# A chunked recurrence with an MLP behind it: another form of the products, three products on GpSimd, all DMAs on SP

## The chip, the cores and the metric

The kernel runs on one core of one Trainium2 chip. The metric is the time of one execution on the device in microseconds, as the median of several runs. A profile of one execution gives the time of each instruction. Its engines are PE (TensorE, matrix products; PEld is its weight load), DVE (VectorE), ACT (ScalarE), POOL (GpSimd) and SP (SyncE, which here only issues DMAs).

## What is computed

Thirty-two heads (4 batches times 8) carry a 40x40 state through 768 steps; the outputs then go through an MLP.

```python
for t in range(S):
    y[:, :, t] = np.einsum('bhd,bhde->bhe', rt, state)
    Sa = np.einsum('bhde,bhe->bhd', state, at)
    state_decay = state * wt[:, :, None, :] - np.einsum('bhd,bhe->bhde', Sa, bt)
    state = state_decay + np.einsum('bhd,bhe->bhde', vt, kt)
...
h = x @ w_in                      # x: [3072, 320], w_in: [320, 2048]
g = h * np.tanh(softplus(h))
out = g @ w_out                   # [2048, 320]
```

## The kernel before

**Chunks.** The 768 steps are cut into 12 chunks of 64 (`C`). Inside a chunk the decays `w` are taken out by running products: `P` (forward) multiplies `a`, `E` (backward, of reciprocals) multiplies `b` and `k`. What is left is a triangular system per head: with A the strictly triangular products of `a` and `b`, and T the inverse of (1 + A), the vectors u = Sa of the whole chunk come from one product with T. The 32 heads lie as two halves (`al`, `be`) on the partitions (0 to 39 and 64 to 103) and eight (`s`) along the row, or as two groups `g` of the recurrence.

**Preparation** (`pre_a`, lines 126 to 203) runs once per chunk and `be`, 24 units in all. SP loads `wa` (decays and `a` in one tile) and `bk`. DVE reduces, inverts and scans (L145 to L157), multiplies `a` by P (L152) and `b`, `k` by E (L170). ACT spreads `a` into block-diagonal `ad` (L155). PE multiplies `bk` by `ad` (L186); ACT evicts the parts into `GP` (L188, L189) and `HA` (L190), DVE masks one part into `HA` (L191) and masks `GP` (L193). PE transposes `bk` (L202). A small product rearranges the chunk's decays into `RW` (L166). POOL stores P (L172).

**Inversion** runs once per pair of chunks. `pre_inv` (L205 to L221) inverts the 32x32 blocks on DVE: a transpose, a loop of 30 steps with a product (L214) and a sum (L216), two more transposes (L218, L220). `post_inv` (L223 to L260) builds the 64x64 inverse from the blocks with 32x32 products (L232, L241), writes it block-diagonally into `bdT` with ACT copies (L249 to L251) and multiplies it into `HA` (L258), evicted as `KT` (L260). T is thus multiplied into the chunk's matrices before the state is known.

**Recurrence.** `step(c)` runs, for two groups g: `step_a` copies the state into `VS` (L279) and gets u in one product with `KT` (L286), evicted into `UVT` (L288); `step_u` transposes u into `UVQ` (L294 with TensorE's transpose, L296 as a product with the identity, L300); `step_d` transposes the state (L310); `step_b` multiplies `UVT` with block-diagonal `r` (`bdr`, L320) and masks into `UVQ` (L322); `step_c` forms outputs and the new state (L340, L345, L348 to L352). Loads of a chunk (`step_loads`, L265 to L273) are into single buffers and are issued behind the chunk before.

**MLP** (`Mlp.run`): 12 blocks of 256 tokens, four quarters each: `mlp1` (L591, L593, L596, L597) and, `LAG` = 3 quarters behind, `mlp2` (L611 to L613). Its weights come as 64-bit numbers and are converted by ACT and DVE (L459 to L469, L500, L501). With `NO1` = 3, three of the eight `w_out` tiles are loaded ahead of the end of the attention and the others after it, when its memory is free.

**Order.** A planner orders the instructions of each engine: by default those written first go first, those that can go are not held back by those that can't, and `high_priority(offset=...)` (the table `OFF`) moves a block forward or back. `ORDER` says in which order the steps of a pair ('0', '1'), the inversion of the next pair ('i') and the preparation two pairs ahead ('a') are written. `QS` names the engines that issue the DMAs: "SGGG" is SP for the loads of the preparation and POOL for step loads, output stores and stores of P. Each engine and each queue runs its list strictly in order.

Of the kernel before, what the change touches and what calls it, by code (L numbers as in the profile page):

```python
# [15 lines left out]
NHA = 8  # L16
# [3 lines left out]
NKT = 2  # L20
# [7 lines left out]
QS = "SGGG"  # L28
NU = 2
NBR = 1  # L30
NAD = 2
# [4 lines left out]
ORDER = '0aiA1'  # L36

OFF = {'I': 80, 'T1': 80, 'P00': -40, 'P10': 80, 'P11': 40, 'b0': 15, 'c0': 600, 'u0': -15, 'u1': 250, 'd0': 250,
       'd1': 150, 'W': 600, 'V': 400, 'E': 150, 'I0': 600, 'I1': -15, 'I2': 15, 'I3': 150, 'I4': 80, 'p4': 15,
       'I5': -150, 'J5': 600, 's0': 150, 's2': -15, 's3': 80, 's4': 250, 's6': -15, 's7': -40, 's8': 150, 's10': -150}  # L40
SORD = 'a0 b0 u0 d0 a1 b1 u1 d1 c0 c1'
# [6 lines left out]
def layouts(inp, S=768):  # L48
# [7 lines left out]
    wt = w.transpose(4, 2, 1, 6, 3, 0, 5).reshape(nch, 2, 2, 40, 8, C)  # L56
    wa = np.zeros(wt.shape[:4] + (1040,), np.float32)
    wa[..., :520].reshape(wt.shape[:4] + (8, 65))[..., 1:] = wt
    wa[..., 528:] = a.transpose(4, 2, 1, 6, 3, 0, 5).reshape(nch, 2, 2, 40, 512)
    o['wa'] = wa  # L60
    bt, kt = (x.transpose(4, 2, 1, 6, 3, 0, 5).reshape(nch, 2, 2, 40, 8, 1, C) for x in (b, k))
    bk = np.concatenate([bt, kt], -2)
    bk[:, 1] = np.concatenate([kt, bt], -2)[:, 1]
    o['bk'] = bk.reshape(nch, 2, 2, 40, 8, 128)
    o['rD'] = np.ascontiguousarray(r.transpose(4, 1, 6, 2, 3, 0, 5)).reshape(nch, 2, 40, 16, C)
    o['vD'] = np.ascontiguousarray(vv.transpose(4, 1, 6, 3, 0, 2, 5)).reshape(nch, 2, 40, 8, 128)
    o['vN'] = np.ascontiguousarray(vv.transpose(4, 2, 5, 3, 0, 1, 6)).reshape(nch, 2, C, 16, 40)
    p = np.arange(128)
    cst = np.zeros((128, 328), np.float32)
    cst[:, :128] = np.eye(128)  # L70
    cst[:, 128:192] = (p[:, None] % 64) < np.arange(64)
    cst[:, 192:256] = np.arange(64) < (p[:, None] // 64) * 32 + p[:, None] % 32
    cst[:, 256:296] = (p[:, None] % 64) == np.arange(40)
    cst[:, 296:328] = np.arange(32) < p[:, None] % 32
# [4 lines left out]
def attention(ctx, tc, I, yD, pD, nch, M):  # L79
# [11 lines left out]
    ci = pool("ci", 1, ictx)  # L91
# [4 lines left out]
    cst = cs.tile([128, 328], F32, name="cst")  # L96
    ident = cst[:, 0:128]
    maskQ = cst[:, 128:192]
    maskH = cst[:, 192:256]
    maskG = cst[:, 296:328]  # L100
    wab = [cp.tile([128, 1040], F32, name=f"wa{i}") for i in range(NWA)]
    bkb = [cp.tile([128, 8, 168], F32, name=f"bk{i}") for i in range(NWA)]
    adb = [cp.tile([128, 8, 2, 2, 32], F32, name=f"ad{i}") for i in range(NAD)] * (2 // NAD)
    d1 = cp.tile([128, 584], F32, name="d1")
    bdT = [ci.tile([128, 8, 2, 64], F32, name=f"bdT{i}") for i in range(2)]
    z = cs.tile([128, 1], F32, name="z")
    V.memset(z, 0.0)
    for w, b in zip(wab, bkb):
        V.memset(w, 1.0)
        G.memset(b, 0.0)  # L110
    for t in [d1] + [x.rearrange("p s k a t -> p (s k a t)") for x in adb[:NAD]]:
        A.copy(t, z.broadcast_to(t.shape))
    for t in bdT:
        G.memset(t, 0.0)
    VS = [cs.tile([128, 2, 344], F32, name=f"VS{be}") for be in range(2)]
    UVT = cs.tile([128, 8, 256], F32, name="UVT")
    UVQ = [cs.tile([128, 16, 104], F32, name=f"UVQ{be}") for be in range(2)]
    bdr = [cs.tile([128, 2, 8, 2, 64], F32, name=f"bdr{i}") for i in range(NBR)] * (2 // NBR)
    ST = [cs.tile([128, 8, 64], F32, name=f"ST{g}") for g in range(2)]
    for t in VS + [UVT] + bdr[:NBR] + ST:  # L120
        G.memset(t, 0.0)

    RW, W2, HA, BKN, GP, KT = {}, {}, {}, {}, {}, {}
    LQ, SQ, OQ, PQ = (dict(S=SP, G=G, A=A)[x] for x in QS)

    def pre_a(c, be):
        n = 2 * c + be
        wa, bk, ad = wab[n % NWA], bkb[n % NWA], adb[n % 2]
        for al in range(2):
            q = slice(al * 64, al * 64 + 40)  # L130
            LQ.dma_start(out=wa[q], in_=I['wa'][c, be, al])
# [255 lines left out]
    def inv(n):  # L387
        with at(tc, 'I%d' % n), at(tc, 'I'):
            TT, T1 = pre_inv(n)
# [276 lines left out]
```

## Time and profile before

| what | value |
|---|---|
| median of 3 runs | 859.57 us (859.17 to 859.66) |
| the profiled execution | 858.42 us |
| its span, first to last instruction | 856.6 us |
| mean granted TensorE clock | 0.95 of full speed |
| busy: PE, DVE, ACT, POOL | 769.2, 466.2, 429.8, 123.5 us |

The time is a little longer than the span, as it includes what lies around the first and last instruction. Busy times add up the moments in which an engine works on something. A row of the groups reads: line, engine, operation, output<-inputs, shapes, count, then busy time in us and the mean of one in ns, then the idle time of the engine before them and what ended it. A busy PE is not PE at its peak, since products overlap; their pace is read from how many start in a stretch.

### The profile page before, as it was taken

To read this page: it belongs to the slowest core of one execution; us is meant where nothing else is said; L and a number is where in the kernel's file an instruction comes from. 1 tells how busy PE (TensorE), PEld (TensorE's weight loads), DVE (VectorE), ACT (ScalarE), POOL (GpSimd) and SP (SyncE) were. 2 spreads that over 40 slices of the span, in tenths; PEclk is the share of its full clock that TensorE was granted. 3 is DMA by queue.
4 is the path that set the end of the run, shared out by engine and by line. 5 is a ranking of instruction groups with operands and counts; after the bars stand their busy time and mean duration, and the time that the engine had idled before them with its cause. 6 is when DMAs were issued, how large, how long until landed. Compare 5 with 4: busy or idle time off the path is not lost.

```text
span 856.6 us, 19033 instructions
## 1 busy us (share of the span) xinstructions
PE 769.2 (90%) x7904; PEld 695.8 (81%) x7904; DVE 466.2 (54%) x975; ACT 429.8 (50%) x937; POOL 123.5 (14%) x206
## 2 busy tenths in 40 slices
PE   2545899899999999998798989999999999999998
PEld 2434777777778777876776889999999999999998
DVE  6789869758758856878663728422221222222110
ACT  4533647674564686557557626433333333333331
POOL 8100022233123213321212200000000000000000
PEclk9855699999979999999899999999999999999999
DMA  5622224443232334423425746201211121100000
GB/s 165 156 70 62 84 56 90 97 115 92 68 103 80 96 86 110 102 64 101 117 81 130 187 97 184 60 18 36 53 39 30 38 54 34 34 20 17 16 1 31
DMA packets 59750, 65.87 MB, mean 77 GB/s; under 512 B 25920, under 2 KB 49472, under 8 KB 59664
## 3 DMA queue, kind: packets, MB, share of 16 engines
q1 hardware_dynamic: 49296, 40.94, 17.2%
q0 software_dynamic: 10368, 23.72, 11.7%
q8 instruction: 62, 1.02, 0.5%
q14 instruction: 24, 0.20, 0.1%
HBM read 52.72 MB, written 11.86 MB: 75 GB/s over the span
## 4 chain that ended last, share of the span: by engine, by line
PE 59%; ACT 9%; DVE 3%; DMA 3%; issue 1%; SPq 0%; DVEq 0%; ACTq 0%
PE ph L591 19%; PE po L611 6%; PE po L612 6%; PE po L613 6%; PE pq L320 3%; PE pa L258 3%; PE pu L296 3%; PE pq L340 2%; PE pa L186 2%; PE pu L294 2%; PE pu L286 2%; PE pq L345 2%; DMA cv_d<-in_wo 2%; PE pu L310 1%; PE pa L202 1%
## 5 line engine op out<-in xcount | busy, mean ns | idle before, releaser
L591 PE MATMUL ph<-xh,w_ih 128*128 128x256 f32 x576 | 148.8, 284 | 0.0
L593 ACT ACTIVATE g<-ph 128x512 f32<-128x512 f32 x96 | 57.1, 597 | 179.0 <-PE ph L591 178.8
L597 DVE TENSOR_TENSOR gl<-g,gh 128x1024 fp32r<-128x1024 f32 x48 | 58.6, 1225 | 160.1 <-ACT gh L596 159.8
L186 PE MATMUL pa<-bk,ad 128*128 128x168 f32 x384 | 86.0, 374 | 46.5 <-DVE bk L170 16.7
L591 PE MATMUL ph<-xh,w_il 128*128 128x256 f32 x576 | 124.0, 283 | 0.0
L611 PE MATMUL po<-w_oh,gh 128*128 128x320 f32 x384 | 118.1, 310 | 1.5 <-ACT w_oh L500 1.5
L612 PE MATMUL po<-w_ol,gh 128*128 128x320 f32 x384 | 118.7, 309 | 0.0
L613 PE MATMUL po<-w_oh,gl 128*128 128x320 f32 x384 | 118.4, 309 | 0.0
L186 PEld LDWEIGHTS pa<-bk,ad 128*128 128x128 f32 x384 | 70.4, 232 | 52.9 <-issue 25.7
L591 PEld LDWEIGHTS ph<-xh,w_ih 128*128 128x128 f32 x576 | 109.5, 190 | 0.2 <-issue 0.2
L591 PE MATMUL ph<-xl,w_ih 128*128 128x256 f32 x384 | 100.6, 284 | 0.0
L591 PEld LDWEIGHTS ph<-xh,w_il 128*128 128x128 f32 x576 | 96.5, 191 | 0.2 <-issue 0.2
L611 PEld LDWEIGHTS po<-w_oh,gh 128*128 128x128 f32 x384 | 71.9, 188 | 2.2 <-ACT w_oh L500 2.2
L591 PEld LDWEIGHTS ph<-xl,w_ih 128*128 128x128 f32 x384 | 73.2, 191 | 0.1
L612 PEld LDWEIGHTS po<-w_ol,gh 128*128 128x128 f32 x384 | 72.2, 188 | 0.1
L613 PEld LDWEIGHTS po<-w_oh,gl 128*128 128x128 f32 x384 | 72.2, 188 | 0.0
L258 PE MATMUL pa<-bdT,HA 128*104 128x128 f32 x384 | 54.1, 294 | 10.4 <-ACT bdT L251 8.2
L216 DVE TENSOR_TENSOR XL<-XL,tmp 128x30 f32<-128x30 f32 (+9 forms) x180 | 59.0, 328 | 2.6
L214 DVE TENSOR_TENSOR tmp<-XL 128x30 f32<-128x30 f32 (+9 forms) x180 | 58.4, 324 | 2.5
L258 PEld LDWEIGHTS pa<-bdT,HA 128*104 128x104 f32 x384 | 47.5, 182 | 14.8 <-ACT bdT L251 9.5
L320 PE MATMUL pq<-bdr,UVT 128*128 128x128 f32 x384 | 51.1, 284 | 2.8 <-DVE UVQ L322 2.3
L596 ACT CAST gh<-g 128x1024 fp32r<-128x1024 f32 x48 | 50.1, 1047 | 1.1
(92 smaller groups left out, 1310.9 us busy)
## 6 DMA issues: line engine op xcount, KB each, us to landing
wa<-in_wa SPq DMA_DIRECT2D x48, 162.5 KB
bk<-in_bk SPq DMA_DIRECT2D x48, 160.0 KB
cv_d<-in_wi SPq DMA_DIRECT2D x12, 512.0 KB
cv_d<-in_wo SPq DMA_DIRECT2D x8, 640.0 KB
pD<-P POOLq DMA_DIRECT2D x48, 81.2 KB, 2.6
VS<-in_vN POOLq DMA_DIRECT2D x24, 160.0 KB, 3.1
UVT<-in_vD POOLq DMA_DIRECT2D x24, 160.0 KB, 3.8
bdr<-in_rD POOLq DMA_DIRECT2D x24, 160.0 KB, 4.9
```

What stands on the lines that cost most here:

```text
L186: PE.matmul(pt[:, j], ad[:, s0 + j].rearrange("p k a t -> p (k a t)"), bk[:, s0 + j], start=(j == 0), stop=True, skip_group_check=True)
L214: V.tensor_tensor(out=tv, in0=X[:, i + 1:32, i:i + 1].broadcast_to([128, 31 - i, i]), in1=X[:, i:i + 1, 0:i].broadcast_to([128, 31 - i, i] ...
L216: V.tensor_tensor(out=X[:, i + 1:32, 0:i], in0=X[:, i + 1:32, 0:i], in1=tv, op=ALU.add)
L258: PE.matmul(pk[:, j], ha[:, s0 + j], bd[:, s0 + j].rearrange("p a t -> p (a t)"), start=(j == 0), stop=True, skip_group_check=True)
L320: PE.matmul(pq[:, s], UVT[:, g * 4 + s, be * 128:be * 128 + 128], br[:, be, g * 4 + s].rearrange("p a t -> p (a t)"), start=(s == 0), stop ...
L591: PE.matmul(o, w, x, start=(j == 0 and n == 0), stop=(n == 7), skip_group_check=True)
L593: A.activation(g[:, f0:f0 + 2], ph, AF.Mish)
L596: A.copy(gh, g)
L597: V.tensor_tensor(out=gl, in0=g, in1=gh.bitcast(F32), op=ALU.subtract)
L611: PE.matmul(po[k], gh[:, j, t], oh, start=(f == 0), stop=False, skip_group_check=True)
L612: PE.matmul(po[k], gh[:, j, t], ol, start=False, stop=False, skip_group_check=True)
L613: PE.matmul(po[k], gl[:, j, t], oh, start=False, stop=(f == 15), skip_group_check=True)
```

## The change

T is no longer multiplied into the chunk's matrices beforehand. `step_a` multiplies the state with `HT` (a by P and the masked products) to W, and `step_u` then multiplies W with T (`TF`), once for u in one layout and once in the other; the transposes of `step_u`, `bdT`, `KT`, `HA`, `ad` and the product for `RW` go. In preparation and in `step_b` the block-diagonal operands go as well: each product uses one half of the partitions (64 rows). DVE's masks of the preparation go from three to two a unit. Products of `a` with P, of `b`, `k` with E and the mask of `GP` move from DVE to POOL, as do copies and clears of `TF`. All DMAs are issued by SP. `OFF` keeps three entries, `ORDER` is '01iaA' (both steps, then inversion, then preparation), and `NO1` is 0: no `w_out` tile is loaded ahead.

```diff
-NO1 = 3
+NO1 = 0
-QS = "SGGG"
+QS = "SSSS"
-ORDER = '0aiA1'
-OFF = {'I': 80, 'T1': 80, 'P00': -40, 'P10': 80, 'P11': 40, 'b0': 15, 'c0': 600, 'u0': -15, 'u1': 250, 'd0': 250,
...
-SORD = 'a0 b0 u0 d0 a1 b1 u1 d1 c0 c1'
+ORDER = '01iaA'
+OFF = {'W': 600, 'V': 400, 'E': 150}
+SORD = 'a0 u0 b0 d0 a1 u1 b1 d1 c0 c1'
...
 # pre_a(c, al)
-        V.tensor_tensor(out=a3, in0=a3, in1=P3[:, :, 0:64], op=ALU.mult)
-        for al in range(2):
-            q = slice(al * 64, al * 64 + 64)
-            A.copy(ad[q, :, :, al], a[q].rearrange("p (s k t) -> p s k t", k=2, t=32))
...
-        V.tensor_tensor(out=bk4, in0=bk4, in1=E3[:, :, 0:64].unsqueeze(2).broadcast_to([128, 8, 2, 64]), op=ALU.mult)
+        for be in range(2):
+            a = ht[hb[be], al, :, be]
+            G.tensor_tensor(out=a, in0=a, in1=P3[hb[be], :, 0:64], op=ALU.mult)
+        bk4 = bk.rearrange("p s (x t) -> p s x t", x=2)
+        G.tensor_tensor(out=bk4, in0=bk4, in1=E3[:, :, 0:64].unsqueeze(2).broadcast_to([128, 8, 2, 64]), op=ALU.mult)
...
-                PE.matmul(pt[:, j], ad[:, s0 + j].rearrange("p k a t -> p (k a t)"), bk[:, s0 + j], start=(j == 0), stop=True,
-                          skip_group_check=True)
...
+        pt = [ps_g.tile([128, 8, 64], F32, name="pa") for _ in range(2)]
+        for s in range(8):
+            for be in range(2):
+                PE.matmul(pt[be][:, s], bk[hb[be], s], ht[hb[be], al, s, be], start=(s == 0), stop=True, skip_group_check=True)
+        for be in range(2):
+            q0, q1 = slice(be * 64, be * 64 + 32), slice(be * 64 + 32, be * 64 + 64)
+            A.mul(gp[q0], pt[be][q0].rearrange("p s (k t) -> p s k t", k=2)[:, :, ::-1], -1.0)
+            A.mul(gp[q1, :, 1], pt[be][q1, :, 32:64], -1.0)
+            V.tensor_tensor(out=ht[hb[1 - be], al, :, be], in0=pt[be][hb[1 - be]],
+                            in1=mask[hb[1 - be]].unsqueeze(1).broadcast_to([64, 8, 64]), op=ALU.mult)
+        G.tensor_tensor(out=gp[:, :, 1], in0=gp[:, :, 1], in1=maskG.unsqueeze(1).broadcast_to([128, 8, 32]), op=ALU.mult)
...
 # pre_inv, behind the loop of L211
+        V.transpose(tf[:, :, 0:32].rearrange("p u t -> p t u"), X)
+        V.transpose(gp[:, :, 1], tf[:, :, 0:32])
+        for be in range(2):
+            q1 = slice(be * 64 + 32, be * 64 + 64)
+            G.tensor_copy(tf[q1, :, 32:64], tf[q1, :, 0:32])
+            G.memset(tf[q1, :, 0:32], 0.0)
...
 # step_loads
+            SQ.dma_start(out=UVT[h * 64:h * 64 + 40, 2 * h:2 * h + 31:2], in_=I['vD'][c, h])
+            SQ.dma_start(out=rT[c % 2][h * 64:h * 64 + 40], in_=I['rT'][c, h])
+            if c > 0:
+                SQ.dma_start(out=bdr[c % 2][h * 64:h * 64 + 40, :, :, h].rearrange("p b s t -> p (b s) t"), in_=I['rD'][c, h])
...
 # step_a
+        for u in range(8):
+            for be in range(2):
+                PE.matmul(pu[hb[be], u], HT[c % NHT][:, u % 2, g * 4 + u // 2, be], VS[be][:, g, u * 40:u * 40 + 40],
+                          start=(u == 0), stop=True, skip_group_check=True)
+        A.mul(W[g][:, 0:320].rearrange("p (u d) -> p u d", d=40), pu, -1.0)
...
 # step_u
+        for u in range(8):
+            t = u0 + u % 2 * 8 + u // 2
+            for be in range(2):
+                PE.matmul(pt[hb[1 - be], u], W[g][hb[be], u * 40:u * 40 + 64], tf[hb[be], t], start=(u == 0), stop=True,
+                          skip_group_check=True)
+            if not last:
+                for be in range(2):
+                    PE.matmul(pn[hb[be], u], tf[hb[be], t], W[g][hb[be], u * 40:u * 40 + 40], start=(u == 0), stop=True,
+                              skip_group_check=True)
+        A.copy(UVT[:, g * 16 + 1:g * 16 + 17:2], pt)
+        if not last:
             for be in range(2):
+                A.copy(UVQ[be][hb[be], g * 8:g * 8 + 8, 64:104], pn[hb[be]])
...
 # step_b
+                t = 2 * (g * 8 + u) + 1 - be
+                PE.matmul(pq[be][:, u], UVT[hb[1 - be], t:t + 2].rearrange("p a t -> p (a t)"), r[hb[1 - be], g * 8 + u],
+                          start=(u == 0), stop=True, skip_group_check=True)
```

`HT` is four buffers, one per chunk, into which the loads put `a` directly; `TF` is two, one per pair. The recurrence's `step_c` and `step_d` are the same products with other index orders.

More of the change, by code (lines that the diff above doesn't have):

```diff
@@ L14 @@
 C = 64
-NHA = 8
+NHT = 4
+NTF = 2
 NBKN = 8
@@ L94, in attention @@
     pw = pool("pw", 2, pctx, "right")
-    cst = cs.tile([128, 328], F32, name="cst")
+    cst = cs.tile([128, 224], F32, name="cst")
     ident = cst[:, 0:128]
[L98 to L103, printed above, removed]
+    mask = cst[:, 128:192]
@@ L288, in step_a @@
[L288 to L297 removed]
+                A.copy(VS[be][srow[be], g].rearrange("p (s d) -> p s d", d=40), st[srow[be], :, 0:40])
@@ L536, in first @@
             self.w_in(wp, cv, range(NQ0, NQ1))
-        if NQ1 == 4:
-            self.mpx = self.pool("mpx", 2)
     def second(self):
```

247 lines of the change are left out of this document (90 added, 157 removed).

## The prediction

> **What bounds the kernel now.** I read the stretches of busy time by stage first, then the chain of waits, then the groups of instructions. The columns are: length, busy time of TensorE, its weight load, DVE, ACT and POOL, the granted clock of TensorE, share and rate of the DMA engines.
>
> ```profile
> span 856.6 us, 19033 instructions
> 0.00:104.00 104.00, 52.68 (x332) 43.94 (x334) 86.58 (x186) 48.83 (x131) 26.37 (x48) 0.74 0.38 106
> 140.00:380.00 240.00, 227.61 (x2901) 185.88 (x2902) 181.83 (x454) 151.65 (x400) 61.47 (x106) 0.97 0.35 90
> 400.00:510.00 110.00, 97.50 (x1361) 82.86 (x1360) 62.74 (x127) 62.78 (x128) 21.79 (x30) 0.95 0.50 123
> 545.00:857.00 312.00, 308.24 (x2336) 307.98 (x2334) 67.96 (x67) 106.28 (x153) 0.00 (x0) 1.00 0.12 32
> ```
>
> There are four stages. In the first, DVE is busy 83% and TensorE half, at a clock of 0.74: preparation of four chunks and the first inversion. From 140 to 380 TensorE is busy 95%, DVE 76%, ACT 63%. From 400 on nothing is prepared any more. From 545 TensorE alone sets the pace of the MLP, which the change leaves alone. The recurrence runs from its first to its last product:
>
> ```profile
> L286 PEld LDWEIGHTS pu<-KT,VS x768: 132/138/232, 108.7 to 491.1; 104*64 104x64 f32 x192
> 508.95 0.61 PE L345 MATMUL pq<-bdr,smd 128*64 128x128 f32 x8
> ```
>
> That is 12 chunks in (509.4 - 108.7), 33.4 us a chunk. By the shares of the 240 us window a chunk holds 31.7 us of TensorE, 25.3 of DVE and 21.1 of ACT. In the steady part TensorE is the bound, and DVE the next.
>
> **TensorE.** The busy time of overlapping products says little, so I take the pace from rows of the chain (start, length, what) and the timeline. One fp32 product is two records.
>
> ```profile
> 326.17 1.91 PE pa L186 x12
> 321.77 1.99 PE pa L258 x16
> 365.90 3.73 PE pq L320 x32
> 402.73 1.11 PE pu L286 x32
> 319.39 1.22 PE pa L241 x64
> 267.18 0.30 PE L294 MATMUL pu<-cst,UVT 128*64 128x128 f32 x1
> 267.77 0.30 PE L294 MATMUL pu<-cst,UVT 128*64 128x128 f32 x1
> ```
>
> A record costs 159 ns at L186, 124 at L258, 117 at L320, 35 at L286 (64 columns, two output halves side by side), 19 at L241 (32x32 pieces), and one turn of the transposes of `step_u` takes 0.59 us. Removed from a chunk: 32 records of L186, 5.1 us; 32 of L258, 4.0; 32 of L320, 3.7; 64 of L286, 2.2; eight turns of `step_u`, 4.7. Sum 19.7 us.
>
> Added: in preparation 64 records of 64 columns, in `step_b` 64 more, each on half of the rows and all columns of the array. No row shows this shape. If the two row halves run side by side as the column halves of L286 do, it is 35 ns; if not, at most the 117 of L320. I take 50, nearer to L286 because the column count is the same: 3.2 us each (2.2 to 7.5). `step_a` has 64 records with 40 columns, at most L286's price: 2.2. `step_u` has 128 records on quarters of the array: between 19 and 35 ns, I take 35, 4.5 us (2.4 to 4.5). Sum 13.1 (9.0 to 21.7). Net -6.6 us a chunk (-10.7 to +2.0): TensorE falls from 31.7 to 25.1 and stops being the bound.
>
> **ACT** loses the block-diagonal copies, the `KT` evictions and the `ad` copies and gains a few evictions. It was busy 63%, so this is worth nothing by itself. If that cover went, the removed `KT` copies of 0.59 us, four a chunk, would be a gain of 2.3 us.
>
> **DVE and POOL.**
>
> ```profile
> L170 DVE TENSOR_TENSOR bk<-bk,wa 128x1024 f32<-128x1024 f32 x24 | 29.2, 1215 | 1.4 <-DMA bk<-in_bk 1.2
> L152 DVE TENSOR_TENSOR wa<-wa,P 128x512 f32<-128x512 f32 x24 | 16.4, 685 | 0.0
> L193 DVE TENSOR_TENSOR GP<-GP,cst 128x256 f32<-128x256 f32 x24 | 10.0, 417 | 4.2 <-ACT GP L189 4.2
> L191 DVE TENSOR_TENSOR HA<-pa,cst 128x192 f32<-128x192 f32 (+1 forms) x72 | 23.8, 331 | 32.6 <-ACT HA L190 31.5 <-PE pa L186 1.0
> L322 DVE TENSOR_TENSOR UVQ<-pq,cst 128x512 f32<-128x512 f32 x48 | 32.8, 687 | 24.6 <-PE pq L320 24.4
> L576 DVE TENSOR_TENSOR xh<-xy,xh 64x256 fp32r<-64x256 f32 x12 | 5.1, 422 | 0.4
> L121 POOL MEMSET bdr<- 128x2048 f32 x1 | 2.1, 2084 | 0.0
> L260 ACT COPY KT<-pa 104x512 f32<-104x512 f32 x48 | 27.4, 586 | 11.2 <-PE pa L258 10.0 <-PE pu L286 0.5
> ```
>
> A unit of preparation (two in a chunk) loses on DVE 1.22 + 0.69 + 0.42 and the three masks of L191, 0.99 together: 3.31 us. It gains two masks of 64x512 out of PSUM. Half the partitions don't halve the time (L576 against L193), so each costs L322's 0.69: 1.37. Net -1.94 a unit, -3.9 a chunk; neighbouring DVE instructions overlap at their ends, about a tenth, so I take -3.5. The transposes of the inversion keep their count and lengths of row. DVE falls from 25.3 to 21.8 us a chunk.
>
> POOL gets, a unit, two products of 512 elements, one of 1024 and one of 256. No POOL product is in the trace. From below: DVE's own rows, 2 x 0.69 + 1.22 + 0.42 = 3.0 us. From above: the memset writes one stream at 1.02 ns an element; two reads and a write one after another would be 3.05, thus 2 x 1.56 + 3.12 + 0.78 = 7.0. I take the middle, 5.0 us a unit, 10 a chunk. With the copies and clears of `TF`, two of each per pair at 2.1 and 1.05 by the same streams, POOL has about 13 us in a chunk: no bound by itself, since units are prepared two pairs ahead of their use. The Trainium skill ("GPSIMD Engine Reference", 3.1 Elementwise) gives 4497 ns for such a product of 2048 elements, from which an estimate is 5.1 us a unit, and the sum would be the same.
>
> What decides is whether a POOL product holds up DVE. Nothing in this trace shows the two at work on SBUF operands together. DVE's time is mostly in instructions with two SBUF operands:
>
> ```profile
> L214 DVE TENSOR_TENSOR tmp<-XL 128x30 f32<-128x30 f32 (+9 forms) x180 | 58.4, 324 | 2.5
> L216 DVE TENSOR_TENSOR XL<-XL,tmp 128x30 f32<-128x30 f32 (+9 forms) x180 | 59.0, 328 | 2.6
> L147 DVE TENSOR_TENSOR_SCAN P<-wa,d 128x520 f32<-128x520 f32 x24 | 29.7, 1236 | 0.3
> L157 DVE TENSOR_TENSOR_SCAN wa<-wa,d 128x519 f32<-128x519 f32 x24 | 29.6, 1235 | 8.1 <-ACT ad L155 8.1
> 260.00:280.00 20.00, 20.00 (x301) 16.78 (x300) 17.71 (x49) 9.23 (x24) 8.16 (x12) 1.00 0.32 85
> 280.00:300.00 20.00, 17.89 (x175) 14.05 (x173) 17.86 (x44) 13.44 (x36) 3.54 (x8) 1.00 0.36 94
> ```
>
> These four groups are 177 us. The hold is therefore between nothing and all of the 10 us a chunk; I take half, since these instructions fill about half of the time in which DVE works. DVE then has 26.8 us a chunk. In its fullest windows of before it reached 17.71 and 17.86 of 20; as the bound I give it 0.87 of the time: 26.8 / 0.87 = 30.8 us a chunk against 33.4, **-2.6 us for eight full chunks, -21 us**. With no hold it is 21.8 / 0.87 = 25.1, with all of it 31.8 / 0.87 = 36.6.
>
> The Trainium skill ("SBUF — State Buffer", SBUF: two separate sides) speaks against the move: DVE and GpSimd share one pair of ports as an exclusive lock, and a DVE instruction with two SBUF inputs and a GpSimd one that reads SBUF shut each other out for a whole instruction. No row of before can test it; taken to its end it is the slower rival below.
>
> **The first stage.** DVE sets it (86.6 of 104 us). Eight units lose 1.94 us each, less a tenth: -14 us. Eight units of POOL at 5.0, half held: +20. POOL also clears more before its first product:
>
> ```profile
> 9.82 0.99 POOL L121 MEMSET ST<- 128x512 f32 x2
> 12.01 0.69 DVE L152 TENSOR_TENSOR wa<-wa,P 128x512 f32<-128x512 f32 x1
> ```
>
> Its clears ended at 10.8 us; four `HT` tiles of 2048 at 2.08, `rT` and `W`, less `bdT` and some of `bk`, move that to about 18, where L152 ran at 12.0. The second scan does not wait for it, so I count 2 of these 6 us. **+8 us** (-12 with no hold, +28 with all).
>
> **The last four chunks** (400 to 510) have no preparation, hence no POOL products. TensorE loses 14.6 and gains 9.9 us a chunk there, -4.7, or -19 in four. Against it the recurrence gets one link more, W and its product: the eviction of W (0.4) and 64 records (2.2), less the shorter `pq`, about 2 us a chunk, +8. **-10 us** (-19 to +8).
>
> **The start of the MLP.** With `NO1` 0 no `w_out` tile is ready before the attention's memory is free.
>
> ```profile
> 516.28 0.31 PE L611 MATMUL po<-w_oh,gh 128*128 128x320 f32 x1
> 515.76 0.81 SPq L459 DMA_DIRECT2D cv_d<-in_wo  x2
> 524.23 0.74 ACT L500 ACTIVATE w_oh<-cv_w 128x640 fp32r<-128x640 f32 x1
> 548.42 3.83 PE ph L591 x32
> ```
>
> The first tile of the late group was ready 9 us after its load was issued, 8 us after `mlp2` first ran. Up to two groups of L591 (3.83 us each) can go in between; I take half of the 8: **+4 us** (0 to +10).
>
> **DMAs on SP.** Five streams move from POOL to SP.
>
> ```profile
> 287.14 1.60 SPq L134 DMA_DIRECT2D bk<-in_bk  x2
> 266.90 0.68 SPq L131 DMA_DIRECT2D wa<-in_wa  x2
> SPq L131 <- DVE bk L170: 130.1, 17, 16.2
> UVQ<-in_vN POOLq DMA_DIRECT2D x24, 160.0 KB, 4.4
> ```
>
> An issue takes 0.34 to 0.80 us; 28 in a chunk are 10 to 22 us of 30.8, so SP has room. But SP stands 130 us in all before loads whose buffer DVE still reads, and now step loads, the `pD` and `yD` stores and the loads of `a` (which wait for `step_a` of four chunks before) stand behind such waits. I price it at 0, because the planner orders them by when they can go and chunks are 30 us apart against 4.4 us of landing. A load of `UVQ` late by an issue and a landing would cost 5 us in a chunk that has no other work.
>
> **Sum:** -21 + 8 - 10 + 4 = -19 us. The profiled execution took 858.4 us (span 856.6 and 1.8 around it), so 839.4; the median of 859.57 is 1.2 above it. Predicted: **840 us**.
>
> **Rivals.** *POOL's products don't hold DVE:* for it speaks only that they work on other tiles. Steady -8.3 x 8 = -67, first stage -12, then -10 and +4: -85, 775 us. *Every product holds DVE for all its length:* for it, DVE's back-to-back inversion loop, which leaves no gap; against it, a POOL product may also fall beside transposes and PSUM masks. Steady +3.2 x 8 = +25, first stage +28, -10, +4: +47, 907 us. It decides from the point where DVE has 33.4 x 0.87 = 29.1 us a chunk, that is 7.3 of the 10 us held. Priorities set by hand on thirty steps are gone as well; if DVE reaches only 0.80 with half the hold, a chunk is 33.5 us and the sum +3. Both together are how it gets slower by 10 to 45 us. *TensorE's clock:* it was 0.74 where TensorE was half idle. At 0.74 for 0.97 the 25.1 us become 32.9, at 95% busy 34.6 a chunk, +10 in eight chunks, and the time is 870. The steady rows with TensorE at 18 of 20 were granted 1.00, so I give it little. *The rewrite moves nothing:* only if all terms cancel.
>
> **Chances.** Half hold (818 to 857) 0.45; no hold or little 0.20; slower by hold, order, SP or clock 0.30; no change 0.05. A measurement of this kernel can tell about 0.2% from no change, 1.7 us. Faster 0.62, same 0.05, slower 0.33 (a little of the main case lies there). The range takes in the free case at 775 and the slower ones to 890; beyond lies the full hold. The likeliest case alone is 818 to 857.
>
> **What would show it.** Right: TensorE in the steady stage well under 95%; DVE the fullest engine; L214 and L216 with maximum lengths or gaps near a POOL product's 1 to 3 us; POOL rows of 1.1, 2.3 and 0.6 us; the row-half products near 35 to 50 ns a record; the MLP from its full pace on unchanged. Wrong: L214 at an unchanged mean beside busy POOL (then the free case), SPq rows as the releaser of recurrence products (then the queue), or a granted clock under 0.9 in the middle (then the clock).

## The result, and the profile after

The changed kernel took 1058.17 us, median of four runs (1054.14 to 1064.01); the kernel before, beside it, 859.62 (859.17 to 861.58). The ratio is 1.231 (1.2246 to 1.2373): slower by 198.5 us, where 840 us was forecast. The profiled execution took 1059.76 us, its span is 1058.0.

Busy time, and the span in 40 slices, of the changed kernel:

```profile
PE 818.9 (77%) x9400; PEld 770.0 (73%) x9400; DVE 490.1 (46%) x879; ACT 339.4 (32%) x621; POOL 179.8 (17%) x163
...
PE   1733888747595687647775567899999999999998
...
DVE  7499373365715581546446584349222222222110
...
PEclk9999966656656555656665665789999999999999
```

No engine stays full before the MLP (slice 27 on): TensorE and DVE take turns, and TensorE's granted clock, 0.9 in the first five slices, is 0.5 or 0.6 in the next twenty. Where the time went is read from the first and last records of the recurrence, and of the MLP's first product, in the changed kernel:

```profile
L250 PE MATMUL pu<-VS,HT x768: 198/230/329, 122.6 to 678.8; 128*64 128x40 f32 x192
L318 PE MATMUL pq<-bdr,smd x352: 272/273/422, 167.1 to 696.1; 128*64 128x128 f32 x176
L562 PE MATMUL ph<-xh,w_ih x576: 279/283/386, 697.7 to 1040.1; 128*128 128x256 f32 x192
```

The recurrence starts at 122.6 us (108.7 before), ends at 696.4 (509.4), and 361.6 us follow (347.2). So the span's 201.4 us more are 13.9 in the first stage, 173.1 in the twelve chunks (47.8 us a chunk, 33.4 before) and 14.4 behind them. The ninth chunk's first product starts at 478.6 us (352.3 before), so the first eight chunks grew by 112.4 us and the last four by 60.7. Three stretches of the time of one pair of chunks show how the engines take turns (columns as in the prediction):

```profile
440.00:460.00 20.00, 11.84 (x80) 9.99 (x80) 10.48 (x15) 5.66 (x13) 9.33 (x7) 0.50 0.23 70
480.00:500.00 20.00, 12.74 (x235) 10.98 (x233) 17.61 (x45) 6.12 (x14) 0.73 (x1) 0.76 0.11 35
520.00:540.00 20.00, 17.92 (x380) 16.36 (x376) 1.29 (x2) 7.12 (x14) 0.00 (x0) 0.50 0.15 47
```

First preparation (all engines half idle), then the inversion (DVE full), then a step in which TensorE is busy 17.92 of 20 us at half its clock while DVE has 1.29 us of work. Before, these three ran beside each other. In the groups (line, engine, operation, form, count, busy time, mean ns, idle time before and what ended it) the changed kernel shows:

```profile
L293 PE MATMUL pq<-rT,UVT 64*128 64x64 f32 x768 | 94.9, 400 | 24.0 <-DVE UVQ L296 14.1 <-DMA rT<-in_rT 6.6 <-ACT UVT L269 3.3
L163 PE MATMUL pa<-HT,bk 64*128 64x64 f32 x768 | 93.3, 420 | 111.5 <-POOL bk L152 77.3 <-POOL bkn L175 22.7 <-DMA bk<-in_bk 11.5
L150 POOL TENSOR_TENSOR HT<-HT,P 64x512 f32<-64x512 f32 x48 | 62.9, 1311 | 62.6 <-DVE P L141 60.7
L152 POOL TENSOR_TENSOR bk<-bk,E 128x1024 f32<-128x1024 f32 x24 | 53.3, 2222 | 13.0 <-DMA HT<-in_a 5.4 <-DMA bk<-in_bk 5.3 <-issue 1.2
L171 POOL TENSOR_TENSOR GP<-GP,cst 128x256 f32<-128x256 f32 x24 | 21.1, 878 | 102.6 <-ACT GP L168 102.4
L141 DVE TENSOR_TENSOR_SCAN P<-w,d 128x520 f32<-128x520 f32 x24 | 38.0, 1583 | 0.7
```

The row-half products L163 and L293 cost 121 and 124 ns a record (93.3 and 94.9 us for 768), not 50. A unit's POOL products take 2 x 1.31 + 2.22 + 0.88 = 5.7 us, and 77.3 us of TensorE's idle time ends with one of them. A scan takes 1583 ns where it took 1236.

### The profile page after: what moved, and what is told of

Same layout as the page of the kernel before. It is cut to its first block, busy times and chain, and to the rows that moved or that the text cites. A ratio compares the mean times of both kernels' runs of the same rounds, so it can differ in the third digit from the quotient of the medians.

```text
span 1058.0 us, 21824 instructions
## 1 busy us (share of the span) xinstructions
PE 818.9 (77%) x9400; PEld 770.0 (73%) x9400; DVE 490.1 (46%) x879; ACT 339.4 (32%) x621; POOL 179.8 (17%) x163
## 4 chain that ended last, share of the span: by engine, by line
PE 56%; DVE 22%; issue 7%; POOL 6%; ACT 5%; DMA 3%; SPq 0%; POOLq 0%; DVEq 0%; ACTq 0%
PE ph L562 15%; PE pq L293 8%; PE po L583 5%; PE po L584 5%; PE po L582 5%; PE pa L163 4%; DVE tmp L191 4%; PE pq L313 4%; DVE XL L193 4%; DVE P L141 3%; POOL HT L150 3%; POOL bk L152 2%; PE pa L223 2%; PE pq L318 2%; DMA cv_d<-in_wo 2%
## 5 line engine op out<-in xcount | busy, mean ns | idle before, releaser
L163 PE MATMUL pa<-HT,bk 64*128 64x64 f32 x768 | 93.3, 420 | 111.5 <-POOL bk L152 77.3
L163 PEld LDWEIGHTS pa<-HT,bk 64*128 64x128 f32 x768 | 88.5, 327 | 119.8 <-POOL bk L152 96.6
L293 PE MATMUL pq<-rT,UVT 64*128 64x64 f32 x768 | 94.9, 400 | 24.0 <-DVE UVQ L296 14.1
L293 PEld LDWEIGHTS pq<-rT,UVT 64*128 64x128 f32 x768 | 90.6, 307 | 28.9 <-DVE UVQ L296 14.7
L296 DVE TENSOR_TENSOR UVQ<-pq,cst 128x512 f32<-128x512 f32 x48 | 31.0, 685 | 134.9 <-PE pq L293 134.9
L179 PE MATMUL pa<-cst,bk 128*128 128x128 f32 x192 | 52.4, 434 | 42.4 <-DVE HT L169 38.8
L169 DVE TENSOR_TENSOR HT<-pa,cst 64x512 f32<-64x512 f32 x48 | 33.0, 688 | 110.9 <-ACT GP L168 110.5
L167 ACT ACTIVATE GP<-pa 32x512 f32<-32x512 f32 x48 | 28.2, 587 | 160.3 <-PE pa L163 159.7
L150 POOL TENSOR_TENSOR HT<-HT,P 64x512 f32<-64x512 f32 x48 | 62.9, 1311 | 62.6 <-DVE P L141 60.7
L179 PEld LDWEIGHTS pa<-cst,bk 128*128 128x128 f32 x192 | 34.2, 216 | 53.3 <-DVE HT L169 45.9
```

The source lines that it names most:

```text
L150: G.tensor_tensor(out=a, in0=a, in1=P3[hb[be], :, 0:64], op=ALU.mult)
L163: PE.matmul(pt[be][:, s], bk[hb[be], s], ht[hb[be], al, s, be], start=(s == 0), stop=True, skip_group_check=True)
L179: PE.transpose(pt[:, j].rearrange("p a b -> p (a b)"), bk[:, s0 + j], ident)
L293: PE.matmul(pq[be][:, u], UVT[hb[1 - be], t:t + 2].rearrange("p a t -> p (a t)"), r[hb[1 - be], g * 8 + u], start=(u == 0), stop=True, ski ...
```

## The experiments

Four causes could have made this: the lost priorities (theory order), SP's in-order queue (theory queue), the three products on POOL with the held port (theory POOL), and TensorE at half clock, whether by the form of its products or by gaps between them (theory clock, with its rival that row halves are slow at any clock). All but the first run are the changed kernel or the kernel before with the edit shown; `SORD` stays as each kernel has it, and `NO1` and the other small edits were not tested alone. Times are of single runs; the kernel before, run beside each group of them, took 853.8 to 863.4 us, so ten microseconds between groups say nothing. "Middle" is the stretch from 200 to 400 us.

**e1: forms of products alone.** A kernel of nothing but products:

```diff
+ for i in range(480): PE.matmul(p[i%2][:, i//2%4, 0:64], w, x[:, 0:64], ...)                # full array
+ for i in range(480): PE.matmul(p[i%2][:, i//2%4, 0:64], w[h[i%2]], x[h[i%2], 0:64], ...)  # row halves in turn
...
```

> This kernel leaves out the whole computation (its output is zeros) and runs stretches of some 480 fp32 products of one form each, with 80 full products of 128 columns ahead of each stretch: full 128x128 weights with 64 columns; row halves (64 rows) with 128 weight columns and 64 columns, the halves in turn; the same with 32 columns; row halves with 64 weight columns and 64 columns; quarters (64 rows by 64 weight columns) with 40 columns; row halves not in turn (240 of one, then 240 of the other); and then 640 full, 640 row-half and 640 quarter products in groups of 16, where each group's weights wait for ScalarE to copy the group before. Theory weights (a record of a 64x128 product lasts as long as its 128 weight columns take to load, whatever its rows): row halves 105 to 118 ns at full clock with 64 columns and the same with 32, about half with 64 weight columns. Theory stream (the 64 columns set the time and the halves don't overlap): 107 ns with 64 columns, 55 with 32, 107 with 64 weight columns. My forecast's price, 50 ns, would show in the second stretch. Theory form (small products lower the clock): row halves and quarters show a granted clock under 0.8 back to back already, the full ones 0.95 or more. Theory gaps (it is the waiting that lowers it): back to back all forms hold 0.95 or more, and the grouped stretches fall, the full ones with the others.

Stretches of it, same columns: full array just after the start and 12 us later; row halves in turn with 64 and with 32 columns, the latter early and late; 64 weight columns; row halves not in turn; then in groups that wait for ScalarE the full array, row halves, and quarters early and late.

```profile
2.00:6.00 4.00, 4.00 (x20) 4.00 (x20) 0.00 (x0) 0.64 (x1) 0.00 (x0) 1.00 0.00 0
14.00:18.00 4.00, 4.00 (x39) 4.00 (x38) 0.00 (x0) 0.00 (x0) 0.00 (x0) 1.00 0.00 0
160.00:170.00 10.00, 10.00 (x184) 10.00 (x182) 0.00 (x0) 0.00 (x0) 0.00 (x0) 1.00 0.01 2
218.75:221.25 2.50, 2.50 (x47) 2.50 (x46) 0.00 (x0) 0.00 (x0) 0.00 (x0) 1.00 0.00 0
270.00:280.00 10.00, 10.00 (x97) 10.00 (x98) 0.00 (x0) 0.00 (x0) 0.00 (x0) 0.50 0.00 0
350.00:360.00 10.00, 10.00 (x350) 10.00 (x348) 0.00 (x0) 0.00 (x0) 0.00 (x0) 1.00 0.02 5
470.00:480.00 10.00, 10.00 (x49) 10.00 (x48) 0.00 (x0) 0.00 (x0) 0.00 (x0) 0.50 0.01 2
740.00:750.00 10.00, 8.79 (x75) 8.51 (x75) 0.00 (x0) 0.83 (x3) 0.00 (x0) 1.00 0.01 2
920.00:930.00 10.00, 8.69 (x78) 8.13 (x78) 0.00 (x0) 0.83 (x3) 0.00 (x0) 0.50 0.00 0
1020.00:1030.00 10.00, 10.00 (x216) 8.99 (x213) 0.00 (x0) 1.67 (x6) 0.00 (x0) 1.00 0.01 3
1060.00:1070.00 10.00, 8.25 (x144) 7.66 (x142) 0.00 (x0) 1.11 (x4) 0.00 (x0) 0.50 0.01 2
```

At full clock row halves in turn cost 10 us / 184 = 54 ns a record: they do run side by side, as I had taken (50). With half the columns it is 53 and with half the weight columns 29, so the weights set the pace, as in theory weights; its price of 105 to 118 ns was wrong, because it left out that the two halves overlap. But the clock is its own story. The stretch of 32 columns fell to 0.50 about 3 us after its start, and the one of halves not in turn lay there too, though TensorE was busy 10 of 10 us in both; the full array kept 1.00 even in groups with an eighth of the time idle; grouped row halves ran at 0.50. The "quarters early" aren't quarters alone: the groups of 1000 to 1040 us show full-array products (L626, of the stretch behind) in their waits.

```profile
L660 PE MATMUL p<-x,w 64*64 64x40 f32 x640 | 22.6, 227 | 0.0
L626 PE MATMUL p<-x,w 128*128 128x128 f32 x136 | 20.7, 290 | 0.0
```

The last of these ran at 1039.5 us; from then on the waits were empty (0.44 us each), and by 1045 us the clock was 0.50. (The stores of the output begin at the same time, so this place alone doesn't isolate it.) Neither theory form nor theory gaps has it alone: full products survive gaps; row halves with 64 columns and quarters hold 1.00 back to back and run at 0.50 with empty waits; and 32 columns, or one half at a time, fall without any wait.

**e2 to e4: products, order.** Three edits, one each:

```diff
- G.tensor_tensor(out=a, ...) / (out=bk4, ...) / (out=gp[:, :, 1], ...)          # e2, after
+ V.tensor_tensor(...)
- ORDER = '01iaA'; OFF = {'W': 600, 'V': 400, 'E': 150}                         # e3, after
+ step 2n, inversion, one chunk's preparation, step 2n+1, the other's; OFF of the kernel before
- ORDER = '0aiA1'; OFF = {'I': 80, ...}                                         # e4, before
+ ORDER = '01iaA'; OFF = {'W': 600, 'V': 400, 'E': 150}
```

> The three elementwise products of the preparation back on VectorE, all else as changed. Theory POOL (the 5.7 us of GpSimd per unit in series, and the port that it holds): the pair of chunks falls from about 120 us by four units times (5.7 - 2.9) = 11 us and the scans return from 1583 and 1704 to about 1236 ns, in all 60 to 90 us: 970 to 1000 us. Theory TensorE (form and clock): 1030 to 1055 us, and the middle of the run still at a clock of 0.5 to 0.67. Theory order (preparation, inversion and steps one after another): about the same, 1020 to 1050 us.

> The changed kernel with the old tuned priorities, and the parts of a pair interleaved as step 2n, inversion of the next pair, preparation of one chunk, step 2n+1, preparation of the other. Theory order: the phases overlap again and the pair falls from about 120 towards 80 us: 880 to 930 us, with the clock back to 0.85 or more. Theory TensorE: the same products in the same shapes, so 1020 to 1060 us with the clock still 0.5 to 0.67 in the middle. Theory POOL: 1040 or more.

> The kernel before with nothing changed but its order: the parts of a pair as in the changed kernel (both steps, then inversion, then preparation), and of the priorities only those of the MLP. Theory order: 970 to 1050 us, most of the 198 us, with a clock under 0.8 in the middle. Theories TensorE and POOL: 860 to 890 us, the clock at 0.85 or more.

e2: 1019.8 us, 38 less, short of the 60 to 90 of theory POOL. e3: 1081.3, 23 more. e4: 861.6 beside 863.4. In the middle of e4:

```profile
200.00:400.00 200.00, 179.59 (x2383) 151.85 (x2384) 155.67 (x399) 125.02 (x330) 52.44 (x89) 0.93 0.36 90
```

My first theory, that the lost priorities made the parts run one after another, falls: the kernel before without them is as fast, with TensorE busy 90% at 0.93. Something else puts preparation, inversion and steps in a row. In the changed kernel, rows of SP's issues and of DVE's work around the stretch of 520 to 540 us (start, length, what, and idle time before it) are:

```profile
513.92 2.59 SPq L239 DMA_DIRECT2D UVQ<-in_vN  x2
516.61 2.04 SPq L349 DMA_DIRECT2D yD<-yev  x2
518.70 1.45 SPq L125 DMA_DIRECT2D w<-in_w  x2
520.19 1.68 SPq L127 DMA_DIRECT2D HT<-in_a  x2
521.98 0.83 SPq L129 DMA_DIRECT2D bk<-in_bk  x2
549.27 0.66 SPq L154 DMA_DIRECT2D pD<-P  x2
```

```profile
532.47 1.29 DVE L296 TENSOR_TENSOR UVQ<-pq,cst 128x512 f32<-128x512 f32 x2 [15.85 <-PE pq L293]
541.62 1.29 DVE L296 TENSOR_TENSOR UVQ<-pq,cst 128x512 f32<-128x512 f32 x2 [7.87 <-PE pq L293]
...
548.01 1.23 DVE L141 TENSOR_TENSOR_SCAN P<-w,d 128x520 f32<-128x520 f32 x1
```

The preparation's loads (L125) come out of SP only at 518.7, behind the last step load (L239) and the results. DVE in turn does the scan of L141 only at 548, behind the step's masks, for which it waits on TensorE; and SP stands from 522.8 to 549.3 at the store of that scan's result, with the next loads behind it.

**e5, e6: a TensorE kept busy.** Ahead of each group of products:

```diff
+ for _ in range(4): PE.matmul(f, fw[:, 0:128], fw[:, 128:128 + f.shape[1]], start=True, ...)   # bf16, 128x128
```

> The changed kernel with added work only: ahead of each group of the attention's products (some 20 groups per chunk) four bf16 products of the full array, whose results the group then overwrites; some 960 of 320 to 512 columns. Nothing is left out. Theory clock (TensorE runs at half speed in the steps because the small products don't use enough of the array): the granted clock in the middle rises from 0.5 to 0.67 to 0.9 or more, the products of L163 and L293 fall from about 115 to about 56 ns per record, and in spite of about 170 us more work on TensorE the run gets shorter, 900 to 1000 us. Theory shape (row halves are slow whatever the clock): more work and no gain, 1100 to 1230 us. Theory POOL: the same as theory shape or a few tens of us more than 1058.

> The same fillers, and the three products of the preparation back on VectorE. If clock and GpSimd are two causes that add up: some 40 to 60 us below the run with the fillers alone, 850 to 950 us. If GpSimd only costs where TensorE is slow: the same as with the fillers alone, within 15 us. If neither holds: 1050 or more.

e5: 1016.3 us, 16 above the range of theory clock; e6: 979.1, above the 850 to 950 expected. In the middle of e5 the clock is 0.97 in place of 0.59:

```profile
200.00:400.00 200.00, 188.87 (x2765) 131.44 (x2764) 123.30 (x248) 67.46 (x146) 57.30 (x51) 0.97 0.32 74
```

With work only added, the run is 42 us shorter, and L163 (L173 there) takes 57.3 us in place of 93.3. So the low clock is a cause and not only a trace of the waiting. And e6 lies 37 below e5, as e2 lay 38 below the changed kernel: the two add up.

**e7, e8, e11, e13: queue and GpSimd, each alone and together.**

```diff
- QS = "SSSS"
+ QS = "SGGG"                                   # e7, after
- V.tensor_tensor(out=a3 / bk4 / gp...)         # L152, L170, L193
+ G.tensor_tensor(...)                          # e8, before
- QS = "SGGG"
+ QS = "SSSS"                                   # e11, before; e13: the edits of e8 and e11
```

> The changed kernel with step loads, results and the stores of the running products issued by GpSimd again, as in the kernel before. Theory queue (in-order waits at SP hold the loads up): 20 to 60 us faster, 1000 to 1040 us. Theories clock and POOL: within 15 us of 1058, or slower, since GpSimd then has both the products and the issues.

> The kernel before with only its three elementwise products of the preparation (L152, L170, L193) moved to GpSimd. My forecast's half-hold: VectorE 21 to 27 us per chunk of work, 830 to 870 us. Theory POOL: the longer chain and the held port cost what they cost in the changed kernel, 30 to 60 us: 890 to 920 us. Theory clock: 850 to 880, the products keep their shapes.

> The kernel before with only its DMA issues all moved to SP. Theory queue (the in-order waits at SP cost by themselves): 920 to 960 us. If they cost only where the steps load more often and wait longer, as in the changed kernel: 860 to 880. My forecast priced it at nothing: 858 to 862.

> The kernel before with both of the small parts: the three products on GpSimd and all issues at SP; the products of TensorE keep their old form. If the two parts add: 858 + 39 + 76 = 965 to 980 us, and the new form with its clock is left with 80 to 95 of the 198 us. If they meet in one chain (each only delays the preparation, and one delay covers the other): 925 to 945. If they explain all: 1030 or more.

e7: 969.9 us, 88 less than the changed kernel, past what even theory queue expected. e8: 897.8 beside 858.5, +39. e11: 930.1 beside 853.8, +76. e13: 976.6 beside 862.4, +114, about the sum of the two (115). Of the 198.5 us, 84 are left for the new form of the products and whatever else changed, when it comes on top of the two.

Waits at SP in e11 (waiting issue, what ended it, us in total, times, longest):

```profile
SPq L172 <- DVE w L150: 53.8, 10, 19.1
SPq L172 <- DVE P L147: 45.2, 4, 22.1
SPq L270 <- PE pq L320: 35.6, 5, 15.1
SPq L267 <- PE pu L286: 30.8, 3, 22.1
```

Such waits stood at POOL before, where other stores and step loads and small clears were behind them. Now the preparation's loads are.

In e8, whole engines and the groups on which the port's hold is read:

```profile
PE 777.3 (87%) x7904; PEld 706.8 (79%) x7904; DVE 474.0 (53%) x903; ACT 428.9 (48%) x937; POOL 223.6 (25%) x278
...
L216 DVE TENSOR_TENSOR XL<-XL,tmp 128x30 f32<-128x30 f32 (+9 forms) x180 | 82.1, 456 | 3.1
```

```profile
L170 POOL TENSOR_TENSOR bk<-bk,wa 128x1024 f32<-128x1024 f32 x24 | 52.9, 2206 | 44.8 <-DVE wa L157 23.3 <-issue 7.2 <-DMA bk<-in_bk 6.7
L152 POOL TENSOR_TENSOR wa<-wa,P 128x512 f32<-128x512 f32 x24 | 28.9, 1204 | 60.0 <-DVE P L147 29.4 <-issue 24.1 <-ACT bdT L250 6.5
L193 POOL TENSOR_TENSOR GP<-GP,cst 128x256 f32<-128x256 f32 x24 | 19.4, 815 | 36.5 <-ACT GP L189 36.5
```

DVE's groups add up to 513.8 us before and 510.1 in e8, though 55.6 (29.2 + 16.4 + 10.0) moved away. So its other instructions got 52 us longer beside 101 us of POOL products: a hold of 0.51 (0.63 by the busy totals 466.2 and 474.0, which count overlapping ends once). The mean of L216 rose from 328 to 456 ns, its longest from 409 to 5311:

```profile
65.23 2.16 POOL L170 TENSOR_TENSOR bk<-bk,wa 128x1024 f32<-128x1024 f32 x1 [2.19 <-issue]
65.49 2.08 DVE L216 TENSOR_TENSOR XL<-XL,tmp 128x150 f32<-128x150 f32 x1
```

This instruction of DVE, 308 ns on the mean before, started behind POOL's product and ended only after it. DVE's work of other kinds kept its length: transposes of L209 2130 ns (2131 before), masks out of PSUM of L322 686 (687). That agrees with what the Trainium skill ("SBUF — State Buffer", SBUF: two separate sides) says of the shared ports, an exclusive lock for the whole instruction against a DVE instruction with two SBUF inputs. By this reading 0.51 is how much of POOL's time met one.

**e14, e15: which issues.** In the changed kernel:

```diff
- QS = "SSSS"      # prep loads, step loads, results, stores of P
+ QS = "SSSG"      # e14
+ QS = "SGSS"      # e15
```

> The changed kernel with only the stores of the running products (L154) issued by GpSimd, the step loads and results left with SP. If it is the stores' waits for VectorE's scans (about 209 us of waits at SP in the changed kernel) that hold up the loads behind them: most of the 88 us, 970 to 1000. If it is the step loads: 1040 to 1060.

> The changed kernel with only the step loads (L232 to L239) issued by GpSimd, stores and results left with SP. If the step loads' waits for TensorE's last readers (about 150 us at SP) hold up the preparation's loads: 970 to 1000 us. If it is the stores: 1040 to 1060. If either alone blocks: both runs stay above 1020.

e14: 1037.8 us, 20 less. e15: 965.1, 93 less: moving the step loads alone gives all that e7 gave. In e15:

```profile
200.00:400.00 200.00, 175.95 (x2494) 159.84 (x2492) 123.86 (x253) 69.98 (x152) 88.80 (x91) 0.62 0.36 81
```

```profile
L163 PE MATMUL pa<-HT,bk 64*128 64x64 f32 x768 | 105.7, 395 | 42.8 <-POOL bkn L175 24.4 <-POOL bk L152 16.6 <-POOL HT L150 1.4
```

TensorE is busy 88% of the middle (66% in the changed kernel: 132.57 of 200), the parts overlap again, yet at a clock of 0.62.

**e9, e10, e12, e16: only the new form left.** Old queues with VectorE's products (e9), with fillers too (e10), with e3's order (e12); old queues, POOL's products and two fillers a group (e16):

```diff
- QS = "SSSS"; G.tensor_tensor(...)
+ QS = "SGGG"; V.tensor_tensor(...)             # e9; e10 + four fillers; e12 + order of e3
- QS = "SSSS"
+ QS = "SGGG"; two fillers                      # e16
```

> The changed kernel with the three products on VectorE and the old division of the DMA issues, so that of the change's three parts only the new form of the products is left (with its order). If the parts add up, 1058 less 38 less 88: 925 to 940 us. If the queue cost only because GpSimd's products were late, or the other way round: 955 to 975. If the new form of the products costs nothing once these two are gone: 830 to 870. The clock in the middle tells what is left: at 0.9 or more the rest is not the clock, at 0.6 to 0.8 it is.

> The same with the four full-array bf16 products ahead of each group. Theory clock: 20 to 60 us below the run without them, so 870 to 910 us. If what is left is TensorE's own work, the fillers' 170 us add to it: 950 or more.

> The new form of the products with VectorE's products and the old issues, and with the parts of a pair interleaved and the old priorities, as in the third run. If the order matters once the queue and GpSimd no longer hold the preparation up: 20 to 60 us below the run without it. If not, within 15 us of it, or up to 25 us above, as it was in the third run.

> The changed kernel with the old division of issues and two, not four, full-array bf16 products ahead of each group (about 85 to 90 us more work for TensorE; nothing left out). Theory clock: below the 970 us of the old division alone, 910 to 950, with the granted clock at 0.9 or more. If two are too few to change the clock: 970 to 1010 with the clock as it was, 0.84.

e9: 994.0 us, e10: 954.9, e12: 1006.4, e16: 956.9. With both small parts undone the kernel is still 140 us slower than the one before, above all three of e9's expectations. So the parts don't add up in the changed kernel: one by one they give back 38 and 88, together 64, and the new form's share is 84 or 140 us by the order in which it is counted. Fillers give 39 in e10 (against e9) and 13 in e16 (against e7), less in time than theory clock had expected of either (870 to 910, 910 to 950). Order again gives nothing (12 more). One result I can't place: e9 is 24 us slower than e7, which differs only in that POOL does the products, though the same move gave 38 with the queue at SP. So POOL's price, +39 in the kernel before, isn't a constant of the changed one.

**e17, e18: is it the clock or the work?** On e15:

```diff
+ four fillers a group                                                      # e17
- PE.matmul(pt[be][:, s], bk[hb[be], s], ht[hb[be], al, s, be], ...)        # e18
+ PE.matmul(pt[be][:, s], bk[:, s], ht[:, al, s, be], ...)                  #   and so in step_b
```

> The changed kernel with the step loads back on GpSimd and four full-array bf16 products ahead of each group (some 170 us more work for TensorE; nothing left out). Theory clock: the clock at 0.93 or more and, since each product is faster, 920 to 955 us against 965 without. If TensorE is already full in this kernel: its added work comes on top, 970 to 1020.

> The changed kernel with the step loads back on GpSimd, and the products of L163 and L293 over all 128 rows instead of over one half of the rows, so that each also sums the other half's operands, which the reference doesn't; the count and the columns stay. By the stretches of the first run a record then takes 112 ns at full clock in place of 56 (halves in turn). Theory clock: these records keep the 112 to 117 ns that they have now at half clock, the other products get faster with a granted clock of 0.9 or more, and the run is no slower, 930 to 970 us. If the clock is not what makes the halves slow: these 1536 records double, 60 to 120 us more, 1010 to 1080.

e17: 983.7 us, 19 more than e15. e18: 1025.0, 60 more, in the range of its other theory (1010 to 1080). In e17 (its L173 is the product L163):

```profile
200.00:400.00 200.00, 177.13 (x2743) 124.97 (x2778) 124.81 (x252) 71.31 (x153) 87.00 (x92) 0.97 0.34 79
```

```profile
L173 PE MATMUL pa<-HT,bk 64*128 64x64 f32 x768 | 51.9, 287 | 20.6 <-POOL bkn L185 12.3 <-POOL bk L161 7.3 <-issue 0.8
```

Theory clock's expectation failed in e17 on the time, in e18 on the clock too. At 0.97 the products did halve (L163 from 105.7 to 51.9 us). Added over the groups of the attention's own products, e17 has 351 us on TensorE where e15 has 525 and the kernel before 470; but the fillers' groups add 244, and once the parts overlap nothing hides that. In e18 full rows did not raise the clock of the middle (0.66), so the row halves alone aren't what lowers it here; their records went from 138 and 120 ns in e15 (L163, L293) to 204 and 181 and did not double, as that other theory had it. Which products lower it, or which of the short waits between them, is open.

All runs of the whole kernel, with the clock granted in the middle:

| products of TensorE | run: us (clock) |
|---|---|
| old form | before: 859.6 (0.96); e4: 861.6 (0.93); e8: 897.8 (0.96); e11: 930.1 (0.90); e13: 976.6 (0.91) |
| new form | changed: 1058.2 (0.59); e2: 1019.8 (0.60); e3: 1081.3 (0.61); e7: 969.9 (0.65); e9: 994.0 (0.64); e12: 1006.4 (0.65); e14: 1037.8 (0.59); e15: 965.1 (0.62); e18, full rows: 1025.0 (0.66) |
| new form, fillers | e5: 1016.3 (0.97); e6: 979.1 (0.95); e10: 954.9 (0.99); e16, two: 956.9 (0.85); e17: 983.7 (0.97) |

The old form holds 0.90 or more even where the queue leaves TensorE idle for 38 of 200 us (e13), the new one 0.66 at most unless fillers are added. That the new form lowers the clock is shown by this; by which of its products, or by which waits between them, is not.

## Why the prediction was wrong

The sum was -19 us; measured +198.5. By its own steps:

- **"I price it at 0" (DMAs on SP)** is the step whose failure is shown best: +76 us alone in the kernel before, 93 of the 198 given back by moving only the step loads away. The reason given, that the planner orders the issues by when they can go and that chunks are 30 us apart against 4.4 us of landing, counted the time of a load and not the place where it stands. SP takes its issues in order, a step load waits for the last reader of a buffer that exists once, and behind it stand the preparation's loads. The prediction named what would stand behind SP's own 130 us of waits (step loads, stores, loads of `a`); what it left out is the reverse, the preparation's loads behind the waits of the step loads and stores.
- **"So I give it little" (TensorE's clock)** is the second: the new form of the products, which brings the clock down, costs 84 to 140 us. The rival had named the clock, but the wrong cause and size: 0.74 taken, 0.59 measured in the middle (0.96 before). The clock was read as a matter of how busy TensorE is, "18 of 20 were granted 1.00"; the changed kernel is busy 17.92 of 20 at 0.50.
- **The row-half price** of 50 ns a record was right at full clock (54 in e1) and wrong in the kernel (121 and 124, above even the 117 taken as the most; 68 and 69 in e17 with fillers). The forecast of a lighter TensorE holds too, but only there: by group sums a chunk's products cost 39.1 us before and 29.3 in e17 (forecast -6.6, measured -9.8), against 44.4 in the changed kernel (533 us over 12). A gain in TensorE's work was turned into a loss by its clock.
- **POOL's half-hold** was right in size (0.51 to 0.63 measured, 0.5 taken; 5.7 us a unit, 5.0 taken), in part by luck: its reason was that two-operand instructions "fill about half" of DVE's working time, and the four groups named are 177 of 466 us, 0.38. Wrong was that it matters only through DVE's total: DVE is busy 46% in the changed kernel, and e8's DVE is no fuller than before (474.0 of 896 us, 466.2 of 856.6). What cost 39 us there must be waits. In e8 the recurrence starts 9.7 us later, 15.2 us of TensorE's idle time stand before L232, 14.7 of them ended by DVE's transpose L218 of the inversion (0.7 before), and 9.1 and 13.8 before the steps' products L320 and L340 (2.8 and 0.6). TensorE's idle time before the preparation's product L186 did not grow (42.3, 46.5 before), though 32.5 of it now ends with POOL. In the changed kernel 77.3 us end with POOL's product of L152. How much is the hold on DVE and how much the longer chain of the preparation is read from the waits and not isolated.
- **"DVE as the next bound"** (-21 us for eight chunks, +112.4 measured): no engine was a bound. The quotient 26.8 / 0.87 supposes that preparation, inversion and steps stay beside each other. That overlap was the hidden assumption, and the queue broke it: with the step loads moved back (e15) TensorE is busy 88% of the middle.
- **The last four chunks** (-10, +60.7 measured; 217.8 us for 157.1) were counted as free of preparation. In the changed kernel the preparation's products run until 591.6 us (383.9 before).
- **Priorities lost**: part of the slower rival; without effect (e4: 861.6 beside 863.4).
- **First stage** +8 forecast, +13.9 measured. **Start of the MLP** +4 forecast; the time behind the recurrence grew by 14.4, in part because before, the MLP's first products ran at 481.9, ahead of the recurrence's end. What `NO1` has of this was not isolated.

Of what I had listed to show it, the clock sign worked ("a granted clock under 0.9 in the middle"), and so did the sign of the hold: the longest instruction of the inversion's sum is 2320 ns (L193; 409 at L216 before). The queue sign didn't: the recurrence's products at L293 have only 6.6 us ended by a DMA, because the queue held the preparation up and the delay came through DVE and POOL. What stays open: which products or waits take the clock down in the kernel, how much the 84 to 140 us of the new form would shrink at full clock without fillers (no run had that), what the 39 us of POOL's products are made of, and why e9 is slower than e7. None of the versions beat the kernel before.

## What to carry to other kernels

When DMA issues change their engine, list what stands behind each waiting issue on the new queue; a load that waits for a buffer's last reader must not stand ahead of the loads of work that is to run beside that reader. A product rewritten into smaller pieces has two prices, at full and at half clock, and the forecast needs a reason why TensorE would keep the clock; being busy isn't one. Before giving an engine's total as the next bound, name what keeps the stages beside each other.

## What the runs showed of the hardware

- TensorE's clock fell to 0.50 while it was busy all the time: in e1 about 3 us after the start of row halves in turn with 32 columns, and in row halves not in turn (204 ns a record). Full products kept 1.00 with an eighth of the time idle; row halves ran at 0.50 in groups with about as much idle and at 1.00 in turn back to back with 64 columns. The Trainium skill ("TensorE: Matmul & The Clock Gate", Part 1: The HAM clock gate) ties the half rate to idle windows of some 3.4 us. The length agrees with this stretch; idleness doesn't, since there was none. The measurement decides.
- The granted clock reads 1.00 at the start of a run while the pace is half: in e1 20 records from 2 to 6 us, 39 from 14 to 18, both at a reading of 1.00. The first stage's clock is better judged by ns a record.
- A full-array fp32 product with 64 columns costs as much as one with 128 (275 ns median each, 92 records in 10 us in both stretches of e1), and 64-row products follow their weight columns: 54 ns for 128, 29 for 64.
- POOL's product of two SBUF operands takes 815 to 878 ns for 256 elements, 1204 to 1311 for 512 and about 2210 for 1024 (e8 and the changed kernel). In e8 it stretched DVE's other instructions by 0.51 of its time, one with two SBUF operands from 0.31 to 2.08 us behind a single product, and left DVE's transposes (2130 ns) and masks out of PSUM (686) as long as they were.
